# Attention and two expert layers on one core: where the second layer's logits copy, one unit's row splits and one unit's transposes stand in the queues

## The chip, the cores and the metric

The kernel runs on one core of a Trainium2 chip. Its time is the device time of one execution in microseconds (us). Before the change three runs gave 878.62, 884.17 and 881.64 us, median 881.64.

## What is computed

Attention over 4 batches, 12 heads, 448 positions and 64 channels, with q and k normalised by their root mean square, gives 1792 token rows of 768 values. Two mixture-of-experts layers follow. Each routes every token to one of 8 experts (768 to 1024 to 768) by the largest logit:

```python
    logits = x @ w_gate                       # second layer: + modality_bias[modality_id]
    e_idx = np.argmax(logits, axis=1)
...
        h = np.maximum(x[mask] @ w1[e], 0.0)
        ye = h @ w2[e]
        out[mask] = gate_w[mask, None] * eom[mask, e, None] * ye   # second layer: without eom
```

## The kernel before the change

**Units.** After attention the tokens stand in a table in order of expert. The kernel works in *units*: up to N tokens of one expert. The first layer has `ua`, `ub` and seven units P0 to P6 with N = 304, 288, 256, 240, 224, 208, 192 (`CAPS`). The second layer has `e2`, `e3` and then `seq`: four wide units B0 to B3 with N = 304 and two remainder units S0, S1 with N = 64, in the order B0, B1, B2, S0, B3, S1. A branch (`If`, L1022) stands in the first of them.

**One unit** (`halves`, L416). Phase 1 has eight steps `fb` 0 to 7: 18 matmuls each (`mm3`, L378: three products of 16-bit halves for 6 slices of the 768 inputs) from the transposed rows `XT` and the first weight (`w1h`, `w1l`) into a PSUM tile `pl`; then ScalarE writes `hh` (L381) and VectorE the remainder `hl` (L382), which also frees the PSUM tile (three in all). Phase 2 has six steps `db` 0 to 5 of 24 matmuls from `hh`, `hl` and the second weight (`w2h`, `w2l`); step db ends in a copy to `yt` (L456), and the transposes of a step (`ytrans`, `pty`, L444) follow one step later in `after`. In the first layer `after` also adds the next layer's logits into the PSUM tile `lgT` (L452).

**Weights.** SyncE loads fp32 slices (`r` for w1, `raw`, `r2a`, `r2b` for w2; L317). ScalarE casts the high half (L310), VectorE subtracts for the low half (L311). A load waits until the earlier slice in its buffer has been split.

**Rows.** GpSimd gathers a unit's token rows into `xr` (L357). `xsplit` (L358) casts the high half on ScalarE into `XS` (L361) and subtracts the low half on GpSimd or VectorE (L362). `xtrans` (L363) is a transposing DMA from `XS` to `XT` on SyncE's queue (L365); a remainder unit has its own `XTx`. `XPLAN` (L501) says at which step of a unit the *next* unit's rows are split on the default engine VectorE (`s`), split with the subtraction on GpSimd (`p`) or transposed (`t`); `late` names the row of that table. With `late=0` all rows are split at step 0 on GpSimd and transposed at step 7.5, between the phases.

**The end of a unit runs inside the next one.** `post` (L468) is a generator: step `do(0)` of the next unit first works through the plan and then takes one piece of it: the last `after`, the scatter of the finished rows (`scatter`, L383, GpSimd), and in the first layer the first piece of `route2` (L485): the copy of `lgT` to `lt` in SBUF (L487, ScalarE). The next pieces follow one step each: logits `lg` on TensorE (L490), the routing arithmetic on VectorE (L494 to L160), the table's scatter (L163).

**Order.** `pin` fixes every engine's instructions in program order. So an instruction that waits holds up all that stand behind it on its engine or queue.

Of the kernel before, what the change touches and what calls it, by code (L numbers as in the profile page):

```python
# [24 lines left out]
def bc(ap, shape):  # L25
    return ap.to_broadcast(shape)

class Moe:
# [366 lines left out]
    def unit(self,u,nx=None,fx=None,side=None,late=0,mid=None,fast={},now=False,fp=0,fr=7,**kw):  # L395

        gen=self.gen(); side=dict(side or {})
        plan=XPLAN[late] if nx is not None else {}
        def do(s):
            if fx is not None and s==fp: self.fetch_pay(fx)  # L400
            for k,t in plan.get(s,()):
                if t<nx.ntl:
                    if k=="t": self.xtrans(nx,t)
                    else: self.xsplit(nx,t,self.nc.gpsimd if k=="p" else None)
            if fx is not None and s==fr: self.fetch_rows(fx)
            for _ in range(fast.get(s,1)): next(gen,None)
            for f in side.pop(s,()): f()
        warm=nx is not None and not nx.same
        for _ in self.halves(u,nx,warm,do,fx,cut=mid is not None,**kw): mid([k for s in plan if s<MID for k in plan[s]])
        for _ in gen: pass  # L410
        for s in sorted(side): do(s)
        if now:
            self.flush()
            if fx is not None: self.fetch_idx(fx)
        elif fx is not None and fr>KF+KD: self.fetch_rows(fx)
    def halves(self,u,nx,warm,do,fx=None,early=True,wfb=None,cut=False):  # L416
        nc=self.nc; N=u.N; pay=self.pays[u.slot]; ntl=u.ntl
        if wfb is None: wfb=0 if N<=128 else 3 if nx is not None and not nx.same and nx.x else 5
        (w2h,w2l),XT=self.planes(u),self.xplane(u)
        xh,xl,hh,hl=[t[:,:,:N] for t in (XT[:,0],XT[:,1].bitcast(BF16),self.hh,self.hl)]  # L420
        r=self.width(u); w1h,w1l=self.planes1(u)
        def w2s():
            self.expert(nx)
            for k in range(KF): self.load_w2(nx,k)
        soon=warm and u.x and not u.same
        for fb in range(KF):
            mid=cut and fb==MID
            if not u.same and not u.x and not mid: self.split_w2(fb,u)
            p=(self.lgp if mid else self.ps.tile([128,512],F32,name="pl1",tag="pl"))[:,:N]
            self.mm3(p,[(w1h[:,k,ts(fb,128)],w1l[:,k,ts(fb,128)],xh[:,k],xl[:,k]) for k in range(KD)],r)  # L430
            if mid: yield; self.split_w2(fb,u)
            do(fb)
            self.relu(p,hh[:,fb],hl[:,fb])
            if soon and fb==1: w2s()
            if warm and nx.x:
                self.expert(nx); self.load_w2(nx,fb)
                if fb>=4: self.split_w2(fb-4,nx)
            if warm and fb==wfb and not nx.w1: self.bring(nx)
        if soon: self.split_w1(0)
        do(7.5)  # L440
        if warm and (u.same or not u.x) and not nx.x: w2s()
        def ytrans(d):
            q=self.pt.tile([128,4,128],F32,name="pty",tag="pt")[:,:ntl]
            for t in range(ntl): nc.tensor.transpose(q[:,t,:],self.yt[:,d,ts(t,128)],self.ident)  # L444
            if u.L.nxt is not None and ntl==2:
                for t in range(ntl): nc.scalar.mul(self.yr[:,t,ts(d,128)],q[:,t],pay[:,t,1:2])
            else: nc.vector.tensor_tensor(out=self.yr[:,:ntl,ts(d,128)],in0=q,in1=bc(pay[:,:ntl,1:2],[128,ntl,128]),op=ALU.mult)  # L447
        Y={}
        def after(d):
            ytrans(d)  # L450
            if u.L.nxt is not None:
                for j in range(2): nc.tensor.matmul(self.lgp[:2*E,:N],u.L.nxt["wgs"][:,d],Y.pop((d,j)),start=(d,j)==(0,0),stop=(d,j)==(KD-1,1))  # L452
        for db in range(KD):
            p=self.ps.tile([128,512],F32,name="pl2",tag="pl")[:,:N]
            self.mm3(p,[(w2h[:,k,ts(db,128)],w2l[:,k,ts(db,128)],hh[:,k],hl[:,k]) for k in range(KF)],r)
            nc.scalar.copy(self.yt[:,db,:N],p)  # L456
            if u.L.nxt is not None:
                yh,yl=[self.st.tile([128,self.NM],F32R,name=n,bufs=2)[:,:N] for n in ("yh","yl")]
                nc.scalar.copy(yh,p); nc.vector.tensor_tensor(out=yl,in0=p,in1=yh.bitcast(F32),op=ALU.subtract)
                Y[db,0],Y[db,1]=yh,yl  # L460
            if db>0: after(db-1)
            if warm and not nx.px: self.warm2(db,None,soon)
            if warm and nx.x:
                if 0<db<5: self.split_w2(db+3,nx)
                if fx is not None and db>2: self.bring(fx,*((0,2),(2,3),(3,4))[db-3])
            do(KF+db)
        if fx is not None and early and not fx.same and not (u.x and fx.x): self.bring(fx,*((4,KD) if warm and nx.x else ()))
        def post():  # L468
            after(KD-1)
            self.scatter(u)  # L470
            if u.L.nxt is not None: yield from self.route2(u,pay[:,:ntl,1:2])
            yield
        self.post=post
# [10 lines left out]
        for k in ((1,) if soon and db==0 else ((0,1),(2,),(3,),(4,),(5,),())[db]): self.split_w1(k,eng=eng if k in (1,3) else None)  # L484
    def route2(self, u, scale):  # L485
        nc=self.nc; R=128; nx=u.L.nxt; sp=self.lp; sm=self.sm; ntl=u.ntl; yt=self.yt; pay=self.pays[u.slot][:,:ntl]; iv=self.ivs[u.slot][:,:ntl]
        nc.scalar.copy(self.lt[:2*E,:u.N],self.lgp[:2*E,:u.N])  # L487
        yield
        lg=sm.tile([128,ntl,E],F32,name="lg2",tag="tp")
        for t in range(ntl): nc.tensor.matmul(lg[:,t,:],self.lt[:2*E,ts(t,128)],self.fold[:2*E],start=True,stop=True)  # L490
        T=lambda n,s=(),dt=F32: sp.tile([128,self.ntl,*s],dt,name="r2_"+n,tag="r2_"+n)[:,:ntl]
        l=T("l",(E,)); b=T("b",(E,)); b2=T("b2",(2,E))
        sh=[128,ntl,E]
        nc.vector.tensor_tensor(out=b2,in0=bc(nx["bias"].unsqueeze(1),[128,ntl,2,E]),in1=bc(pay[:,:,2:4].unsqueeze(3),[128,ntl,2,E]),op=ALU.mult)  # L494
        nc.vector.tensor_tensor(out=b,in0=b2[:,:,0],in1=b2[:,:,1],op=ALU.add)
        nc.vector.tensor_tensor(out=l,in0=lg,in1=bc(scale,sh),op=ALU.mult)
        nc.vector.tensor_tensor(out=l,in0=l,in1=b,op=ALU.add)
        yield
        yield from self.route_g(sp,sm,l,ntl,R,nx["ohsum"],nx["ord"],iv=iv,pay=pay,tag="tp",lag=True)

XPLAN={5:{1:[("s",1),("t",0)],2:[("s",2),("t",1)],3:[("t",2)]},7:{9:[("s",0),("t",0)]},4:{0:[("p",0)],2:[("t",0),("t",1),("t",2)]},6:{1:[("t",0),("t",1),("t",2)]},0:{0:[("p",0),("p",1),("p",2)],7.5:[("t",0),("t",1),("t",2)]},3:{3:[("s",0)],4:[("s",1)],5:[("s",2)],7.5:[("t",0),("t",1),("t",2)]},  # L501
1:{8:[("s",0),("s",1),("s",2),("t",0),("t",1),("t",2)]},
    2:{7.5:[("s",0),("s",1),("s",2),("t",0),("t",1),("t",2)]},None:{10:[("s",0),("t",0)]}}
class LazyUnit:
# [329 lines left out]
def body_full(tc,q,k,v,g_q,g_k,wg,wog,w1,w2,mod,wg2,bias2,v1,v2,out,stop=False,O=None):  # L834
    nc=tc.nc
    with ExitStack() as ctx:
        M=Moe(tc,ctx)
# [120 lines left out]
        def stepper(name):  # L958
            def f():
                if name not in S: S[name]=F[name]()  # L960
                next(S[name],None)
            return f
# [18 lines left out]
        sides={1:{KF+j:[stepper("table1")] for j in range(6)},2:{7:[stepper("pick2")]*2,**{j:[stepper("pick2")] for j in range(8,14)}},3:{7:[stepper("pick3")]*2,**{j:[stepper("pick3")] for j in range(8,14)}}}  # L981
        for g in range(7): M.unit(P[g],nx=P[g+1],fx=P[g+2],side=sides.get(g),late=0 if g else 3)
        e2,e3=S["e2"],S["e3"]
# [14 lines left out]
            yield from M.chunks(S["s2"],lp,ns,off3,c,NS,E)  # L998
        F.update(table2=table2,table3=table3)
        t2=stepper("table2")  # L1000
        M.unit(e2,nx=e3,side={j:[t2] for j in (7,8,9,10,11)})
        M.unit(e3,nx=B0,fx=S["B"][1],side={0:[lambda: M.fetch_pay(B0)],2:[lambda: M.fetch_rows(B0)],**{KF+i:[stepper("table3")] for i in range(6)}},late=1,fp=8,fr=9)
        seq=S["B"][:3]+[S["S"][0],S["B"][3],S["S"][1]]
        (be,nbi),(se,nsi)=S["b2"],S["s2"]
# [28 lines left out]
            return f  # L1033
        def known(): S["over"]=load(over,E+G2+G1)
        def px(t): return lambda: M.xsplit(seq[4],t,nc.gpsimd)
        sides={0:{0:[more],3:[known]},2:{KF+3+t:[px(t)] for t in range(3)},4:{KF+1:[nc.gpsimd.drain]}}
        for u in seq: u.own=True
        for j,u in enumerate(seq):
            nx,fx=seq[j+1] if j<5 else None,seq[j+2] if j<4 else None
            M.unit(u,nx=nx,fx=fx,side=sides.get(j),late={2:4,3:6,4:4}.get(j,0),mid=others(u,nx,fx) if j==0 else None)  # L1040
        M.flush()
        pin(tc,mark)

# [28 lines left out]
```

## Time and profile before

| | |
|---|---|
| median of three runs | 881.64 us |
| the profiled execution | 877.29 us |
| its span | 875.6 us |
| PE busy | 817.9 us (93%) |
| VectorE (DVE) busy | 649.3 us (74%) |
| ScalarE (ACT) busy | 545.0 us (62%) |
| GpSimd (POOL) busy | 389.9 us (45%) |
| mean granted TensorE clock | 0.98 |

The profiled execution's 877.29 us is 1.69 us over its span and 4.35 us under the median of the three runs. Attention takes about the first 300 us of the span, the first expert layer the stretch to about 610 us, the second the rest.

### The profile page before, as it was taken

Reading aid. Unit: us, or ns where it says so; the run is one execution under the profiler, and the core shown is the slowest. Engines: PE = TensorE matmul, PEld = TensorE weight load, DVE = VectorE, ACT = ScalarE, POOL = GpSimd, SP = SyncE. Lnnn points to the kernel's source line nnn. Section 1 sums busy time; section 2 is a strip of 40 time slices with the busy share of each in tenths; the row PEclk is TensorE's granted clock in tenths of the full one; section 3 lists DMA queues with packets and bytes.
Section 4 is the critical chain, followed back from the end, with each engine's and each line's share of the span. In section 5 each row is a group of like instructions: output and inputs, shape, how many; then the busy total and the mean of one; then the engine's idle time right before and its main releaser. Section 6 shows DMA issues by size and latency. Waiting matters only on the chain. (4 is left out here: it accounts for less than half of the span.)

```text
span 875.6 us, 23286 instructions
## 1 busy us (share of the span) xinstructions
PE 817.9 (93%) x8881; PEld 640.0 (73%) x8898; DVE 649.3 (74%) x1302; ACT 545.0 (62%) x1039; POOL 389.9 (45%) x397
## 2 busy tenths in 40 slices
PE   4698999998998899899999999999999999999897
PEld 1265666665665588777889999988677768878676
DVE  6689889888778775786797767776676846577674
ACT  4577777776776654655556686776545535456563
POOL 5677777876776623131424333344402524024301
PEclk9799999998999989999999999999999999999999
DMA  5567665766465482979486797898677759896961
GB/s 137 130 152 183 162 155 162 201 161 163 114 172 142 143 229 77 278 290 326 105 321 145 275 320 201 249 348 239 204 251 280 235 108 332 192 315 207 291 245 52
DMA packets 142137, 181.42 MB, mean 207 GB/s; under 512 B 71944, under 2 KB 109592, under 8 KB 142016
## 3 DMA queue, kind: packets, MB, share of 16 engines
q1 hardware_dynamic: 134048, 157.06, 62.9%
q0 software_dynamic: 6656, 22.32, 7.8%
q8 instruction: 71, 1.16, 0.6%
q10 hardware_dynamic: 1312, 0.47, 0.2%
q14 instruction: 50, 0.41, 0.2%
HBM read 129.73 MB, written 23.94 MB: 176 GB/s over the span
## 5 line engine op out<-in xcount | busy, mean ns | idle before, releaser
L378 PE MATMUL pl<-XT,w1h 128*128 128x304 f16 (+6 forms) x1236 | 210.5, 275 | 4.9 <-PEq L1022 2.0
L378 PE MATMUL pl<-hh,w2h 128*128 128x304 f16 (+7 forms) x720 | 194.4, 275 | 0.0
L378 PE MATMUL pl<-hh,w2l 128*128 128x304 f16 (+7 forms) x720 | 194.1, 274 | 0.0
L378 PE MATMUL pl<-hl,w2h 128*128 128x0 bf16 x720 | 187.9, 264 | 3.0 <-DVE hl L382 3.0
L378 PE MATMUL pl<-XT,w1l 128*128 128x304 f16 (+6 forms) x618 | 172.5, 279 | 0.0
L680 POOL TENSOR_TENSOR plo<-p 128x448 f16<-128x448 f32 x142 | 140.3, 1005 | 56.1 <-ACT p L677 52.4
L378 PEld LDWEIGHTS <-w1h 128*128 128x128 f16 x1536 | 134.5, 98 | 27.4 <-ACTq L1022 2.3
L378 PEld LDWEIGHTS <-w2h 128*128 128x128 f16 x1440 | 134.0, 98 | 24.6 <-issue 1.4
L311 DVE TENSOR_TENSOR w1l<-r,w1h 128x1024 bf16<-128x1024 f32 x90 | 109.7, 1233 | 46.5 <-ACT w1h L310 46.5
L456 ACT COPY yt<-pl 128x304 f32<-128x304 f32 (+8 forms) x102 | 36.6, 358 | 117.2 <-PE pl L378 117.2
L362 POOL TENSOR_TENSOR XS<-xr,XS 128x768 bf16<-128x768 f32 (+5 forms) x27 | 46.8, 1749 | 130.4 <-ACT XS L361 100.6
L381 ACT ACTIVATE hh<-pl 128x304 f16<-128x304 f32 (+8 forms) x135 | 49.1, 364 | 81.0 <-PE pl L378 69.5
L677 ACT ACTIVATE p<-pst,eb 128x896 f32<-128x896 f32 (+1 forms) x96 | 86.5, 911 | 14.8 <-PE pst L673 13.9
L310 ACT CAST w1h<-r 128x1024 f16<-128x1024 f32 x90 | 93.5, 1056 | 0.1
L690 PE MATMUL av<-vv,p 128*128 128x65 f16 (+1 forms) x768 | 89.8, 199 | 1.8 <-ACT xrow L702 1.8
L690 PEld LDWEIGHTS <-p 128*128 128x128 bf16 (+1 forms) x768 | 73.5, 102 | 20.8 <-issue 15.0
L692 PE MATMUL av<-vv,plo 128*128 128x65 f16 (+1 forms) x768 | 88.0, 196 | 0.6 <-DVE plo L680 0.6
L691 PE MATMUL av<-vv,p 128*128 128x64 f16 (+1 forms) x768 | 88.5, 198 | 0.0
L654 DVE TENSOR_REDUCE m<-psm 128x2 f16<-128x896 f32 x70 | 76.0, 1086 | 9.1 <-PE psm L649 7.3
L378 PEld LDWEIGHTS <-w1l 128*128 128x128 bf16 x768 | 74.1, 98 | 11.8
L378 PEld LDWEIGHTS <-w2l 128*128 128x128 bf16 x720 | 70.3, 98 | 16.7 <-issue 4.1
L382 DVE SCALAR_TENSOR_TENSOR hl<-pl,hh 128x304 bf16<-128x304 f32 (+8 forms) x135 | 53.5, 398 | 34.8 <-ACT hh L381 34.4
(328 smaller groups left out, 1806.3 us busy)
## 6 DMA issues: line engine op xcount, KB each, us to landing
r<-in_moe_w_dram SPq DMA_DIRECT2D x96, 512.0 KB, 8.9
raw<-in_moe_w_dram SPq DMA_DIRECT2D x64, 384.0 KB, 5.9
r2a<-in_moe_w_dram SPq DMA_DIRECT2D x32, 384.0 KB, 6.8
r2b<-in_moe_w_dram SPq DMA_DIRECT2D x32, 384.0 KB, 8.9
T<-Z SPq DMA_DIRECT2D x48, 224.0 KB, 3.8
T<-Z SPq DMA_DIRECT2D x48, 112.0 KB, 2.9
yd<-zero SPq DMA_DIRECT2D x14, 384.0 KB, 3.1
rv<-in_v_dram SPq DMA_DIRECT2D x24, 192.0 KB, 4.2
```

What stands on the lines that cost most here:

```text
L310: if part!=1: nc.scalar.copy(h,t)
L311: if part!=0: (eng or nc.vector).tensor_tensor(out=l,in0=t,in1=h,op=ALU.subtract)
L362: if part!=0: (eng or nc.vector).tensor_tensor(out=self.XS[:m,t,1].bitcast(BF16),in0=x,in1=h,op=ALU.subtract)
L378: self.nc.tensor.matmul(o,a,b,start=i==0,stop=i==tot-1); i+=1
L381: nc.scalar.activation(h,p,AF.Relu)
L382: nc.vector.scalar_tensor_tensor(out=l,in0=p,scalar=0.0,in1=h,op0=ALU.max,op1=ALU.subtract)
L654: if t<3: nc.vector.tensor_reduce(m[:,t:t+4:3],p[:,:,:S],axis=AX.X,op=ALU.max,negate=True)
L677: self.nc.scalar.activation(self.d["P",i][:,self.u(kt)],p[:,:nn,:S],AF.Exp,bias=self.eb,scale=0.125)
L680: eng.tensor_tensor(out=self.d["L",i][:,u],in0=P[:,u],in1=self.hi(P)[:,u],op=ALU.subtract)
L690: nc.tensor.matmul(o,hh,w[:,0:65],start=kt==0,stop=False)
L691: nc.tensor.matmul(o[:,0:64],hh,w[:,65:129],start=False,stop=False)
L692: nc.tensor.matmul(o,ll,w[:,0:65],start=False,stop=kt==3)
```

## The change

It has three parts.

1. `post` copies `lgT` to `lt` itself, as a piece of its own, and `do(0)` takes that piece *before* the plan. The last `after` comes with it. A later call takes the scatter and, in the first layer, route2's first piece, as before.
2. `e2` gets `late=3` in place of 0: the rows of `e3` are split at steps 3, 4 and 5 with the subtraction on VectorE, instead of at step 0 on GpSimd. The transposes stay at step 7.5.
3. B3's rows are split on GpSimd at steps db 2, 3 and 4 of B2 instead of 3, 4 and 5, and each tile is transposed one step after its split, still in B2. Before, the three transposes stood at step 1 of S0 (`XPLAN[6]`); S0's plan is now empty (`XPLAN[8]`).

```diff
@@ unit
         def do(s):
             if fx is not None and s==fp: self.fetch_pay(fx)
+            if s==0: next(gen,None)
             for k,t in plan.get(s,()):
@@ halves
         def post():
             after(KD-1)
+            if u.L.nxt is not None: nc.scalar.copy(self.lt[:2*E,:N],self.lgp[:2*E,:N])
+            yield
             self.scatter(u)
             if u.L.nxt is not None: yield from self.route2(u,pay[:,:ntl,1:2])
             yield
@@ route2
-        nc.scalar.copy(self.lt[:2*E,:u.N],self.lgp[:2*E,:u.N])
         yield
@@ XPLAN (of the line, the entry that differs)
-6:{1:[("t",0),("t",1),("t",2)]}
+8:{}
@@ body_full
-        M.unit(e2,nx=e3,side={j:[t2] for j in (7,8,9,10,11)})
+        M.unit(e2,nx=e3,side={j:[t2] for j in (7,8,9,10,11)},late=3)
...
-        sides={0:{0:[more],3:[known]},2:{KF+3+t:[px(t)] for t in range(3)},4:{KF+1:[nc.gpsimd.drain]}}
+        def tx(t): return lambda: M.xtrans(seq[4],t)
+        sides={0:{0:[more],3:[known]},2:{KF+2:[px(0)],KF+3:[px(1),tx(0)],KF+4:[px(2),tx(1)],KF+5:[tx(2)]},4:{KF+1:[nc.gpsimd.drain]}}
...
-            M.unit(u,nx=nx,fx=fx,side=sides.get(j),late={2:4,3:6,4:4}.get(j,0),mid=others(u,nx,fx) if j==0 else None)
+            M.unit(u,nx=nx,fx=fx,side=sides.get(j),late={2:4,3:8,4:4}.get(j,0),mid=others(u,nx,fx) if j==0 else None)
```

ScalarE at the start of P6 (N = 192), before. `XS<-xr` are the casts of e2's three row tiles, `yr` the end of P5, `hh` P6's first phase.

```order
L310 CAST w2h<-raw_118 128x768
L361 CAST XS<-xr_78 128x768
L361 CAST XS<-xr_79 128x768
L361 CAST XS<-xr_80 48x768
L446 ACTIVATE yr<-pty,pay_84 128x128 x2
L487 COPY lt<-lgT 16x208
L381 ACTIVATE hh<-pl_10098 128x192
```

The same place now:

```order
L310 CAST w2h<-raw_118 128x768
L447 ACTIVATE yr<-pty,pay_84 128x128 x2
L471 COPY lt<-lgT 16x208
L361 CAST XS<-xr_78 128x768
L361 CAST XS<-xr_79 128x768
L361 CAST XS<-xr_80 48x768
L381 ACTIVATE hh<-pl_10098 128x192
```

The casts of the rows now stand behind `yr` and `lt`, and `hh` stays last. The same holds at the starts of P1 to P5, with two row tiles (in P1 and P2 without `yr`, which VectorE writes for three tiles).

GpSimd at the start of e2, before (`xr` are e3's rows, `yd` the rows that P6 has finished):

```order
L357 DMA xr_80<-yd,idx_87 48x768
L362 TENSOR_TENSOR XS<-xr_78,XS 128x768
L362 TENSOR_TENSOR XS<-xr_79,XS 128x768
L362 TENSOR_TENSOR XS<-xr_80,XS 48x768
L387 DMA yd<-yr,idx_85 1792x768 x2
```

VectorE in phase 1 of e2 now, steps 2 to 5:

```order
L382 SCALAR_TENSOR_TENSOR hl<-pl_10713,hh 128x304
L311 TENSOR_TENSOR w2l<-raw_119,w2h 128x768
L362 TENSOR_TENSOR XS<-xr_78,XS 128x768
L382 SCALAR_TENSOR_TENSOR hl<-pl_10750,hh 128x304
L311 TENSOR_TENSOR w2l<-r2a,w2h 128x768
L362 TENSOR_TENSOR XS<-xr_79,XS 128x768
L382 SCALAR_TENSOR_TENSOR hl<-pl_10776,hh 128x304
L311 TENSOR_TENSOR w2l<-r2a,w2h 128x768
L362 TENSOR_TENSOR XS<-xr_80,XS 48x768
```

The three subtractions have left GpSimd's queue, where the scatter of P6 stood behind them, and stand between the `hl` and `w2l` of VectorE. ScalarE's three casts have moved to the same steps.

SyncE's queue at the end of B2, before. The loads `r_0` to `r_5` of B3's first weight stand in a row; these are the last of them and what follows (`pay` is for S1, `raw` is B3's second weight):

```order
L317 DMA r_5_75<-in_moe_w_dram 128x1024
L321 TENSOR_LOAD s2gi
L321 ISA x2
L345 ISA
L345 DMA pay_81<-o_1132 64x4
L365 DMA_TRANSPOSE XT<-XS 128x12x128 x2
L365 DMA_TRANSPOSE XT<-XS 128x12x48
L317 ISA
L317 DMA raw_118<-in_moe_w_dram 128x768
```

The same place now, from `r_1` on:

```order
L317 DMA r_1_71<-in_moe_w_dram 128x1024
L365 DMA_TRANSPOSE XT<-XS 128x12x128
L317 ISA
L317 DMA r_2_72<-in_moe_w_dram 128x1024
L365 DMA_TRANSPOSE XT<-XS 128x12x128
L317 ISA
L317 DMA r_3_73<-in_moe_w_dram 128x1024
L365 DMA_TRANSPOSE XT<-XS 128x12x48
L317 ISA
L317 DMA r_4_74<-in_moe_w_dram 128x1024
L317 ISA
L317 DMA r_5_75<-in_moe_w_dram 128x1024
```

The transposes now stand ahead of the loads `r_2`, `r_3` and `r_4`, which they had stood behind.

## Rows read from the trace of the kernel before

**Rows 1.** Waits of PE, whole span: us in total, times, longest.

```profile
PE pl L378 <- DVE hl L382: 4.0, 9, 0.7
...
PE lg L490 <- ACT lt L487: 3.8, 3, 2.2
```

**Rows 2.** Timeline of PE at e2's start: start, duration, in brackets idle before.

```profile
615.28 0.61 PE L490 MATMUL lg<-fold,lt 16*128 16x8 f32 x4 [2.17 <-ACT lt L487]
```

**Rows 3.** Timeline of PE: phase 2 of P3 and of P6 waits for hl.

```profile
503.93 0.24 PE L378 MATMUL pl<-hl,w2h 128*128 128x0 bf16 x1 [0.35 <-DVE hl L382]
...
595.95 0.24 PE L378 MATMUL pl<-hl,w2h 128*128 128x0 bf16 x1 [0.66 <-DVE hl L382]
```

**Rows 4.** Timeline of ACT: start of P3, and the casts at P6.

```profile
487.79 1.58 ACT L361 CAST XS<-xr 128x768 f16<-128x768 f32 x2
489.25 0.63 ACT L446 ACTIVATE yr<-pty,pay 128x128 f32<-128x128 f32 x2
489.76 0.34 ACT L487 COPY lt<-lgT 16x256 f32<-16x256 f32 x1
...
579.17 2.31 ACT L361 CAST XS<-xr 128x768 f16<-128x768 f32 x3
```

**Rows 5.** Timeline of PE: the last transposes, at P3 and at P6.

```profile
488.01 0.38 PE L444 MATMUL pty<-ident,yt 128*128 128x128 f32 x2
...
579.17 0.38 PE L444 MATMUL pty<-ident,yt 128*128 128x128 f32 x2
```

**Rows 6.** Timeline of POOL at the start of P3.

```profile
488.74 3.27 POOL L362 TENSOR_TENSOR XS<-xr,XS 128x768 bf16<-128x768 f32 x2 [9.21 <-ACT XS L361]
```

**Rows 7.** Timeline of DVE in phase 1 of P3.

```profile
491.12 1.70 DVE L311 TENSOR_TENSOR w2l<-raw,w2h 128x768 bf16<-128x768 f32 x1 [0.31 <-ACT w2h L310]
...
493.66 0.95 DVE L311 TENSOR_TENSOR w2l<-raw,w2h 128x768 bf16<-128x768 f32 x1
```

**Rows 8.** Timeline of ACT at the start of e2.

```profile
612.95 1.57 ACT L361 CAST XS<-xr 128x768 f16<-128x768 f32 x2 [1.30 <-DMA xr<-yd,idx]
...
614.93 0.29 ACT L487 COPY lt<-lgT 16x192 f32<-16x192 f32 x1
```

**Rows 9.** Timeline of PE at the start of e2: the last logits.

```profile
610.52 0.25 PE L452 MATMUL lgT<-yl,wgs 128*16 128x192 f32 x1
```

**Rows 10.** Stretches: length, PE, PEld, DVE, ACT, POOL busy (instructions), PE clock, DMA, GB/s.

```profile
616.00:632.70 16.70, 16.70 (x134) 12.67 (x133) 13.18 (x38) 7.65 (x15) 6.24 (x5) 1.00 0.48 166
821.00:822.00 1.00, 1.00 (x6) 0.59 (x5) 0.78 (x2) 0.31 (x1) 0.00 (x0) 0.50 1.03 402
```

**Rows 11.** Timeline of PE at B3's start.

```profile
820.14 0.68 PE L378 MATMUL pl<-XT,w1h 128*128 128x304 f16 x2 [1.92 <-DMA XT<-XS]
```

**Rows 12.** Timeline of POOL in B2 and S0.

```profile
803.22 2.08 POOL L362 TENSOR_TENSOR XS<-xr,XS 128x768 bf16<-128x768 f32 x1 [9.43 <-ACT XS L361]
806.58 3.78 POOL L362 TENSOR_TENSOR XS<-xr,XS 128x768 bf16<-128x768 f32 x2 [1.28 <-ACT XS L361]
```

**Rows 13.** Timeline of SyncE's queue: loads of B3's w1, then the transposes.

```profile
792.99 13.74 SPq L317 DMA_DIRECT2D r<-in_moe_w_dram  x6
...
808.19 7.70 SPq L365 DMA_TRANSPOSE XT<-XS  x3
```

**Rows 14.** Timeline of DVE in S0 and B3.

```profile
816.16 0.29 DVE L447 TENSOR_TENSOR yr<-pty,pay 128x128 f32<-128x128 f32 x1 [0.81 <-DMA out_dram<-yr,idx]
...
820.37 1.22 DVE L311 TENSOR_TENSOR w1l<-r,w1h 128x1024 bf16<-128x1024 f32 x1
```

**Rows 15.** Timeline of ACT at B3's start.

```profile
817.16 1.09 ACT L310 CAST w1h<-r 128x1024 f16<-128x1024 f32 x1
...
824.10 0.42 ACT L381 ACTIVATE hh<-pl 128x304 f16<-128x304 f32 x1 [0.85 <-PE pl L378]
```

**Rows 16.** DMA issues from 785 to 830 us: KB each, median us to landing.

```profile
r<-in_moe_w_dram SPq DMA_DIRECT2D x6, 512.0 KB, 5.3
...
XT<-XS SPq DMA_TRANSPOSE x3, 8.9
```

More of the change, by code (lines that the diff above doesn't have):

```diff
@@ L499, in route2 @@
         yield from self.route_g(sp,sm,l,ntl,R,nx["ohsum"],nx["ord"],iv=iv,pay=pay,tag="tp",lag=True)
-XPLAN={5:{1:[("s",1),("t",0)],2:[("s",2),("t",1)],3:[("t",2)]},7:{9:[("s",0),("t",0)]},4:{0:[("p",0)],2:[("t",0),("t",1),("t",2)]},6:{1:[("t",0),("t",1),("t",2)]},0:{0:[("p",0),("p",1),("p",2)],7.5:[("t",0),("t",1),("t",2)]},3:{3:[("s",0)],4:[("s",1)],5:[("s",2)],7.5:[("t",0),("t",1),("t",2)]},
+XPLAN={5:{1:[("s",1),("t",0)],2:[("s",2),("t",1)],3:[("t",2)]},7:{9:[("s",0),("t",0)]},4:{0:[("p",0)],2:[("t",0),("t",1),("t",2)]},8:{},0:{0:[("p",0),("p",1),("p",2)],7.5:[("t",0),("t",1),("t",2)]},3:{3:[("s",0)],4:[("s",1)],5:[("s",2)],7.5:[("t",0),("t",1),("t",2)]},
 1:{8:[("s",0),("s",1),("s",2),("t",0),("t",1),("t",2)]},
```

## The prediction

> **What bounds the kernel now.** I read the page first: PE is busy 93% of the span, so only work or waits on PE's path can move the time, and after that the waits of PE. Two groups of them bear on the change: 3.8 us in three waits for `lt`, and 4.0 us in nine for `hl` [rows 1]. The longest wait for `lt`, 2.17 us, stands at e2's start [rows 2]; the other two (1.6 us together) stand at P5's and P6's starts.
>
> Then the timeline, stage by stage. Phase 2 of P3 waits 0.35 us for VectorE's last `hl`, that of P6 0.66 us; P4 and P5 lie between [rows 3]. So in these four units VectorE sets the end of phase 1: its chain runs without a gap from the second step on. What PE wins back earlier in such a unit it loses to that `hl`, and what delays VectorE there delays PE in full. The other place is B3's start, where PE waits 1.92 us for the transposed rows [rows 11].
>
> **Part 1, the copy of the logits ahead of the casts.** At P3 the two casts start at 487.79; `yr` and `lt` follow at 489.25 and 489.76 [rows 4]. Now `yr` and `lt` come first. They need the last transposes, which end at 488.39 [rows 5]. Two `yr` take 0.51 us (489.25 to 489.76), `lt` about 0.25 (from 489.76 to where `hh` is begun), so the first cast starts at 488.39 + 0.75 = 489.14, 1.35 us later. GpSimd's two subtractions, which end at 488.74 + 3.27 = 492.01 [rows 6], follow it. That matters because VectorE's `w2l` at 491.12 takes 1.70 us where the same operation a step later takes 0.95 [rows 7]: it ends 0.81 us after GpSimd does, as if it had waited for GpSimd's end. So GpSimd's end starts VectorE's chain, and the chain has no slack. I charge P3 with the whole 1.35 us.
>
> At P6 the casts start at 579.17 [rows 4], the transposes end at 579.55 [rows 5]: 579.55 + 0.75 − 579.17 = 1.13. P4 and P5 by the same arithmetic come to 1.29 and 1.20. Sum 1.35 + 1.29 + 1.20 + 1.13 = 5.0. In P2 the casts move 2.1 us, but `hl` has some 1.8 us of room there; I take 0.2. P1 and the earlier units are covered by their room. Part 1 in P1 to P6: **+5.2 us**. Its own gain there, the two shorter waits for `lt` (1.6 us), is worth nothing, since `hl` comes last. Bounds: 0, if GpSimd's delay finds VectorE busy with something else; 7, if P2 pays in full.
>
> At e2 the copy is free to start when the last logits end, 610.52 + 0.25 = 610.77 [rows 9]; before, it stood at 614.93 behind casts that waited for the gather of rows [rows 8]. The copy thus ends near 611.4, 3.8 us sooner, and the wait of 2.17 us [rows 2] is gone entirely: **−2.2 us**. The bounds are 0, if something else of the same length is late there, and 2.2.
>
> **Part 2, e3's rows on VectorE.** It adds three subtractions of 0.95 us (the duration of the like `w2l`, [rows 7]), 2.85 us, to e2's phase 1. In that stretch VectorE is busy 13.18 of 16.70 us [rows 10], so 3.52 us are free and PE didn't wait for `hl`. I cost it at nothing; the cover is thin, and gone if the freed start moves phase 1 closer to VectorE. Then up to 2.2 us return as a wait for the last `hl`. GpSimd loses 5 us of work off the path; the casts cost ScalarE nothing that PE waits for.
>
> **Part 3, B3's rows.** Before, the splits run at 803.22 and from 806.58 to 810.36 [rows 12], and the three transposes issue from 808.19 on, for 7.70 us, behind all six loads [rows 13]. One step of B2 is about 3.36 us (806.58 − 803.22), so the first split now starts near 799.9, the second and third where the first and second stood, at 803.2 and 806.6; at 1.9 to 2.1 us each they end near 802, 805.3 and 808.4. With the slowest landing in the trace, 8.9 us [rows 16], the last transpose is in at 808.4 + 8.9 = 817.3, before S0's last matmul (820.14 − 1.92 = 818.2 [rows 11]). The 1.92 us go; what is late next is the low half of B3's first weight: VectorE's last `w1l` ends at 820.37 + 1.22 = 821.59 [rows 14]. Ahead of it `yr` waited 0.81 us for the scatter [rows 14], which GpSimd now issues about 1.3 us sooner; so 820.78. Three matmuls of 0.13 us behind it end the first step at 821.2. Before, `hh` of that step began at 824.10 [rows 15]: after the wait the granted clock stood at 0.50, the 1.2 GHz level [rows 10]. The gain is 824.1 − 821.2 = **−2.9 us**.
>
> The cost is in SyncE's queue. The loads `r_2` to `r_5`, issued until 792.99 + 13.74 = 806.73 before [rows 13], now stand behind transposes that wait for GpSimd. The third can't issue before 808.4, so `r_5` goes at about 812. With 5.3 us [rows 16] it lands at 817.3; its cast stood at 817.16 [rows 15], and the chain of `w1l` gives it another microsecond or two. I charge nothing, and nothing for `pay` and the second weight's loads, which stay behind. As the upper bound, `r_5` waits for the last transpose to land and then takes 5.3 us: 817.3 + 5.3 = 822.6, cast 1.09, `w1l` 1.22, matmuls 0.39: 825.3, that is +1.2.
>
> This last order is also what a page speaks of. The Trainium skill, "DMA: Bandwidth & Descriptors", section "Queues, rings and completion order", says that on each DMA engine the descriptors of one queue are consumed in ring order, so a load behind a transpose can't overtake it. By it `r_5` would land some 1.4 us after the third transpose, at 818.7, and the first step would end at 821.4: a gain of 2.7 instead of 2.9. No run here shows it yet.
>
> **Sum.** 5.2 − 2.2 − 2.9 = +0.1. The profiled execution took 877.29, so 877.4; it lies 4.35 under the median of the runs shown, 881.64, and I forecast against that median: **881.7**.
>
> **Rivals.**
>
> 1. *The later casts cost VectorE nothing.* VectorE's `w2l` gets in between GpSimd's two subtractions, and the chain fits. For it: P1's and P2's chains have room. Against it: the 1.70 against 0.95 in P3 [rows 7], and waits for `hl` at all four ends. −2.2 − 2.9 = −5.1: 876.5.
> 2. *Slower: the queue.* The place is SyncE between `r_1` and `r_5`; the price is `r_5` landing up to 822.6. It decides from about 818.5 on, where the last `w1l` no longer hides it. Then part 3 gives +1.2 instead of −2.9: +4.2, 885.8. For it: the transposes take 7.70 us of the queue's time [rows 13]. Against it: DMA has free time in S0.
> 3. *Part 3 changes nothing:* the clock falls there anyway, or the weight comes as late as the rows did. 5.2 − 2.2 = +3.0: 884.6. For it: `w1l` ends only 1.45 us after PE's present restart at 820.14.
> 4. *Part 2 takes e2's gain back:* +2.3, 883.9.
>
> **Numbers.** Chances: forecast 0.50, rivals 0.17, 0.15, 0.13, 0.05. The range takes in all of them, 876.5 to 885.8, and something over a microsecond at either end, since the three runs of before alone lie 5.6 us apart: **875 to 887**. One per cent, 8.8 us, is about what a measurement can tell from no change; no case reaches it by itself. Faster by more than 1%: 0.04; within it: 0.91; slower: 0.05.
>
> **What would show it.** In the profile after: no wait for `lt` at e2; the first cast of P3 some 1.3 us later within the unit and its `w2l` of the second step longer by as much, with `hl` waits of 1.5 to 2 us at the starts of phase 2 of P3 to P6 in place of 0.2 to 0.7 (if they stay as they are, rival 1 holds); an e2 without a wait for `hl`; at B3 no wait for the rows, a granted clock of 1.00, and `r_5` landing before 818.5 on the old time. The forecast is wrong if VectorE's chain in P3 to P6 has room that the waits don't show, or if B3's start keeps its wait under another name.

## The result and the profile after

Six runs of the changed kernel gave a median of 890.07 us, six of the kernel before 879.15: a ratio of 1.0139, 95% interval 1.011 to 1.0169. A second comparison (below) gave 1.0091, interval 1.0061 to 1.012. The change makes the kernel slower by about 1%. The forecast was no change (881.7, range 875 to 887); the time measured lies 3 us above that range.

The profiled execution took 889.20 us, its span 887.5. Read first the waits of PE (total, times, longest), against [rows 1]:

```profile
PE pl L378 <- DVE hl L382: 16.4, 14, 7.4
```

The waits for `hl` rose from 4.0 to 16.4 us. Of the rise, 7.4 us are one wait in S0, and 5.0 lie in P2 to P6 (2.4 before, 7.4 now). The waits for `lt` (3.8 us) are gone, and so is the wait for the rows at B3. The timeline of PE tells where the new ones stand (start, duration, idle before in brackets); one row each of P3, P4, P5, P6, and the longest, in S0:

```profile
501.62 0.34 PE L378 MATMUL pl<-XT,w1h 128*128 128x240 f16 x2 [0.69 <-DVE hl L382]
...
534.46 0.34 PE L378 MATMUL pl<-XT,w1h 128*128 128x224 f16 x2 [0.94 <-DVE hl L382]
...
565.96 0.33 PE L378 MATMUL pl<-XT,w1h 128*128 128x208 f16 x2 [1.19 <-DVE hl L382]
...
598.11 0.32 PE L378 MATMUL pl<-XT,w1h 128*128 128x192 f16 x2 [1.97 <-DVE hl L382]
...
827.44 0.19 PE L378 MATMUL pl<-hl,wxh 128*128 128x0 bf16 x1 [7.40 <-DVE hl L382]
```

**The start of P3,** all engines, against [rows 4], [rows 6] and [rows 7]:

```profile
495.43 0.34 ACT L471 COPY lt<-lgT 16x256 f32<-16x256 f32 x1
495.68 1.56 ACT L361 CAST XS<-xr 128x768 f16<-128x768 f32 x2
496.59 3.23 POOL L362 TENSOR_TENSOR XS<-xr,XS 128x768 bf16<-128x768 f32 x2 [8.93 <-ACT XS L361]
...
498.25 2.39 DVE L311 TENSOR_TENSOR w2l<-raw,w2h 128x768 bf16<-128x768 f32 x1 [0.31 <-ACT w2h L310]
```

P3 now begins at 492.75 (486.28 before), so the casts stand 2.93 us into the unit, 1.42 later than before. `w2l` of the second step starts 0.66 us later within the unit, takes 2.39 us instead of 1.70, and ends at 500.64, 0.82 us after GpSimd (499.82), just as before (0.81).

**The start of e2,** PE, against [rows 2]: the logits no longer wait.

```profile
624.56 0.61 PE L492 MATMUL lg<-fold,lt 16*128 16x8 f32 x4
```

**S0,** VectorE and SyncE's queue, against [rows 13] and [rows 14]:

```profile
819.30 0.20 DVE L351 TENSOR_SCALAR iv<-pos,s2gc 128x1 f32<-128x1 f32 x1
827.09 0.16 DVE L352 TENSOR_TENSOR idx<-pay,iv 128x1 int32<-128x1 f32 x1 [7.58 <-DMA pay<-o]
827.17 0.22 DVE L382 SCALAR_TENSOR_TENSOR hl<-pl,hh 128x64 bf16<-128x64 f32 x1
```

```profile
809.46 1.47 SPq L365 DMA_TRANSPOSE XT<-XS  x1
811.18 0.71 SPq L317 DMA_DIRECT2D r<-in_moe_w_dram  x1
812.92 2.19 SPq L365 DMA_TRANSPOSE XT<-XS  x1
815.35 0.71 SPq L317 DMA_DIRECT2D r<-in_moe_w_dram  x1
816.38 1.21 SPq L365 DMA_TRANSPOSE XT<-XS  x1
817.83 1.13 SPq L317 DMA_DIRECT2D r<-in_moe_w_dram  x2
819.79 0.55 SPq L345 DMA_DIRECT2D pay<-o  x1
```

The same load of `pay` before the change:

```profile
807.53 0.55 SPq L345 DMA_DIRECT2D pay<-o  x1
```

This is the cause in three steps. `pay`, the 64 rows of the table that S1's gather needs, is issued behind `r_5`, which stands behind transposes that wait for GpSimd. It goes at 819.79, 5.0 us after S0's first product (814.80); before, it went 0.3 us after it (807.53 and 807.24). VectorE works out S1's row numbers (`idx`, L352) at step 7 of S0's first phase and waits 7.58 us for it. S0's last `hl` stands behind `idx` on VectorE, and phase 2 needs that `hl`.

B3's start itself came out as forecast: no wait for the rows, and the granted clock at 1.00, the 2.4 GHz level, where it stood at 0.50 [rows 10]. Stretches of the changed kernel (columns as there), the second in S0's phase 2 after the wait:

```profile
834.00:835.00 1.00, 1.00 (x9) 0.76 (x8) 1.00 (x3) 0.59 (x1) 0.00 (x0) 1.00 0.37 110
...
828.00:829.00 1.00, 1.00 (x22) 0.94 (x20) 0.61 (x2) 1.00 (x3) 0.62 (x1) 0.50 1.04 418
```

**Where the 11.9 us between the two spans lie.** A unit is counted from PE's first product in it to that of the next:

| us | P0's start | P0 to end | P2 to P6 | e2 | S0 + B3 | S1 |
|---|---|---|---|---|---|---|
| before | 372.58 | 502.99 | 156.18 | 42.24 | 53.06 | 15.27 |
| changed | 378.83 | 508.64 | 161.45 | 40.00 | 57.76 | 14.91 |

6.25 us lie ahead of P0, and all of them ahead of `ua` (which starts at 317.38 and 323.69), in the attention, which the change doesn't touch. From P0 on: +5.27 in P2 to P6, −2.24 in e2, +4.70 in S0 and B3, −1.71 in B0 (which holds the branch), −0.36 in S1. B0's part isn't the change's: a second trace of the kernel before (below) has 41.25 us there, like the changed kernel's 41.27, and not 42.98. The 4.70 are 7.40 for the new wait, less 1.92 for the rows' wait and 1.45 in B3, plus 0.7 in the rest of S0.

### The profile page after: what moved, and what is told of

Same layout as the page of the kernel before. It is cut to its first block, busy times and chain, and to the rows that moved or that the text cites. A ratio compares the mean times of both kernels' runs of the same rounds, so it can differ in the third digit from the quotient of the medians.

```text
span 887.5 us, 23272 instructions
## 1 busy us (share of the span) xinstructions
PE 822.2 (93%) x8881; PEld 643.0 (72%) x8898; DVE 655.9 (74%) x1305; ACT 546.0 (62%) x1039; POOL 382.1 (43%) x394
## 5 line engine op out<-in xcount | busy, mean ns | idle before, releaser
L378 PE MATMUL pl<-XT,w1h 128*128 128x304 f16 (+6 forms) x1236 | 208.0, 273 | 8.5 <-DVE hl L382 5.7
L362 POOL TENSOR_TENSOR XS<-xr,XS 128x768 bf16<-128x768 f32 (+5 forms) x24 | 41.4, 1740 | 125.9 <-ACT XS L361 108.7
L692 PEld LDWEIGHTS <-p 128*128 128x128 bf16 (+1 forms) x768 | 74.3, 103 | 21.2 <-issue 15.4
L693 PEld LDWEIGHTS <-p 128*128 128x128 bf16 (+1 forms) x768 | 75.5, 104 | 2.0 <-issue 1.0
```

Of the source, the lines that this page charges most:

```text
L362: if part!=0: (eng or nc.vector).tensor_tensor(out=self.XS[:m,t,1].bitcast(BF16),in0=x,in1=h,op=ALU.subtract)
L378: self.nc.tensor.matmul(o,a,b,start=i==0,stop=i==tot-1); i+=1
L692: nc.tensor.matmul(o,hh,w[:,0:65],start=kt==0,stop=False)
L693: nc.tensor.matmul(o[:,0:64],hh,w[:,65:129],start=False,stop=False)
```

## The experiments

**The parts one by one.** Four kernels on one chip. In all four TensorE's small products of S0 and S1 had four or five gaps, most of 0.4 to 0.6 us and some 0.75 us apart (S1 took 18.3 to 19.7 us in place of 15), and the kernel before ran at a median of 887.24 beside them; so the ratios within the set count, and stage against stage within it. (P4 to P6 have a few such waits too, of 0.4 to 0.9 us.) None of the four came out at its expected time from P0's start to the end: 510.3, 507.0, 514.4 and 508.6 us against about 506, 500.8, 505.7 and 500.5.

Part 1 alone (`e2` with late=0, B3's rows as before):

> Part 1 alone: the logits copy ahead of the casts everywhere; e2's rows plan and B3's rows as before the change. Theory: the later casts move GpSimd's row subtractions, and with them VectorE's chain, by 1.1 to 1.6 us in each of P2 to P6, +5.3 us in all, and the wait for lt at e2 goes, -2.2: from P0's start to the end +3 us against before (503.0). Rival, that the loss in P2 to P6 needs part 2 or 3: about -2. If the slower attention of the changed kernel (P0 starts at 378.8 in place of 372.6) comes from part 1, P0 starts near 379 here.

Ratio 1.0047 (1.0014 to 1.0081). P2, P3, P5 and P6 took 34.79, 32.94, 30.66 and 31.24 us, as in the changed kernel, so the loss there needs neither part 2 nor 3 (P4 took 32.25 against 31.63, which isn't explained). The wait for `lt` at e2 is gone; e2 took 40.56, as PE waits 0.39 us for `hl` there. P0 started at 378.67.

Part 2 alone:

```diff
-        M.unit(e2,nx=e3,side={...})
+        M.unit(e2,nx=e3,side={...},late=3)
```

> Part 2 alone: e3's rows split on VectorE at steps 3 to 5 of e2. Theory: lt at e2 no longer stands behind the casts, since these have left step 0; -2.2 us from P0's start to the end (503.0 before), and P2 to P6 as before. Rival, that only the copy's move wins it: 0. P0 starts within a few us of 372.6 if the attention's time is not the change's.

Ratio 0.9986 (0.9954 to 1.0018), which leaves the sign open. In the trace e2 takes 39.99 us against 42.24, and the wait for `lt` is gone. But this trace alone doesn't show that part 2 won it. Part 3 alone and part 3 with `pay` early (next) have neither part 1 nor part 2; the first has the same row as part 2 alone, the second waits 1.88 us:

```profile
621.37 0.61 PE L490 MATMUL lg<-fold,lt 16*128 16x8 f32 x4
...
620.53 0.61 PE L490 MATMUL lg<-fold,lt 16*128 16x8 f32 x4 [1.88 <-ACT lt L487]
```

In the fourteen traces the wait is absent from all eight with part 1 or part 2, and lasts 0 to 2.17 us in the six with neither (0.8 on average): the casts ahead of the copy wait for the gather of the rows. So either part takes the wait away, and what that is worth changes from run to run. P2, P3 and P4 are as before (34.58, 31.59, 30.34).

Part 3 alone, and part 3 with `pay` early:

> Part 3 alone: B3's rows split and transposed sooner. Theory: pay for S1 is issued on SyncE after the transposes and r_5, lands some 7 us after VectorE's idx wants it, and hl of S0 stands behind idx: a PE wait of 7 us for hl in S0, the rows' wait of 1.9 and the half clock after it gone, +2.7 us from P0's start to the end. My forecast before the result: -2.9. Rival, that the late loads r_2 to r_5 hold S0: the wait is the same with pay early (next kernel).

```diff
-2:{KF+2:[px(0)],...
+2:{KF+1:[lambda: M.fetch_pay(seq[5])],KF+2:[px(0)],...
-M.unit(u,nx=nx,fx=fx,...
+M.unit(u,nx=nx,fx=fx,...,fp=99 if j==3 else 0)     # no second fetch in S0
```

> Part 3 alone, with pay for S1 issued on SyncE at step db 1 of B2, ahead of the loads of B3's first weight. Theory: no wait for hl in S0; the last weight slice lands about 1 us later than its chain wants, so B3's first step ends 2 to 3 us sooner than before the change: -2.5 us from P0's start to the end, and 5 us under the kernel with part 3 alone. Rival, the loads r_2 to r_5 themselves are too late: S0 or B3's start waits 3 us or more for w1h or w1l, 0 to +2 us.

Part 3 alone: ratio 1.0065 (1.0031 to 1.0098). With `pay` early: 0.9975 (0.9942 to 1.0008). The same instruction on VectorE, first without and then with the early issue:

```profile
825.23 0.16 DVE L352 TENSOR_TENSOR idx<-pay,iv 128x1 int32<-128x1 f32 x1 [5.23 <-DMA pay<-o]
```

```profile
819.91 0.16 DVE L352 TENSOR_TENSOR idx<-pay,iv 128x1 int32<-128x1 f32 x1
```

S0 takes 19.83 and 14.58 us, B3 38.70 in both; PE's wait for `hl`, 4.71 us without the early issue, is gone with it. Moving one load of 1 KB takes 5.25 us out of S0, and with it all of part 3's loss; the late loads `r_2` to `r_5` themselves, which both kernels have, hold nothing of that size (in a faster S0 the last of them does cost 0.9 us: see the version with parts 2 and 3 and `pay` early, below). My rival 2 had the right queue and the wrong victim. The gain over a kernel without part 3 is small in this set (S0 and B3 took 53.6 with part 1 or part 2 alone, 53.28 here), since the slow S0 hides B3's rows anyway.

**Both kernels again.**

> The kernel before, profiled a second time. If the attention's time (P0 starts at 372.6 in the first trace, 378.8 in that of the changed kernel, 376 to 379 with one part alone) is a matter of when TensorE's granted clock falls after the same waits, it starts P0 elsewhere than at 372.6 here, up to 379; if the change slows the attention, at 372.6 within 1 us. From P0's start to the end 503 us, and some 2 us more in S0 and S1 if the gaps of TensorE seen there in the runs with one part alone belong to the chip or the run.

> The changed kernel again. By the parts measured alone (part 1 +4.2, part 3 +5.8, with part 2 adding nothing since part 1 wins the same wait) +8 to +10 us against before; by the stages of the two traces +5.7; by the first comparison +10.9.

The kernel before, a second time: P0 starts at 375.51, and from there to the end it takes 501.47 us. P2 to P6 agree with the first trace to 0.06 us. Two waits don't: the logits at e2 wait 0.67 in place of 2.17, and the rows at B3 2.32 in place of 1.92:

```profile
616.79 0.61 PE L490 MATMUL lg<-fold,lt 16*128 16x8 f32 x4 [0.67 <-ACT lt L487]
...
820.19 0.68 PE L378 MATMUL pl<-XT,w1h 128*128 128x304 f16 x2 [2.32 <-DMA XT<-XS]
```

The changed kernel: 887.83 (11 runs) against 879.51 (28 runs), ratio 1.0091 (1.0061 to 1.012); P0's start 377.37, P0 to end 508.83, P2 to P6 161.24, S0 and B3 57.87. So the stages from P0 on cost 5.7 us in the first pair of traces and 7.4 in the second, and 7.4 in both when B0 is left out.

P0's start differs by run, not by edit. In the fourteen traces it lies between 372.1 and 378.8, and the two last versions below, whose code is the same up to P0's second phase, stand at 372.25 and 376.96. The waits there are alike; TensorE's granted clock is not. Stretches of the first 300 us, before and changed (length, busy times of PE, PEld, DVE, ACT, POOL with instructions, PE clock, DMA, GB/s):

```profile
80.00:100.00 20.00, 17.72 (x227) 12.05 (x226) 18.80 (x30) 14.69 (x27) 15.39 (x16) 1.00 0.71 180
...
0.00:300.00 300.00, 267.31 (x3328) 174.94 (x3329) 247.50 (x437) 210.35 (x382) 213.01 (x263) 0.97 0.62 157
```

```profile
80.00:100.00 20.00, 17.72 (x205) 11.61 (x204) 17.32 (x28) 12.90 (x22) 14.71 (x14) 0.91 0.76 190
...
0.00:300.00 300.00, 266.43 (x3244) 171.98 (x3245) 245.22 (x431) 208.10 (x378) 211.50 (x262) 0.95 0.62 154
```

In the first pair both wait 1.98 us at 87 to 88 us; the changed kernel goes on at the 1.2 GHz level for a while, the other doesn't. The mean of the first 300 us is 0.97 against 0.95. The second profile of the kernel before has 0.95 too. All fourteen traces fall in line: by their clock records TensorE stood at the 1.2 GHz level for 20 to 41 us ahead of `ua`, and `ua` starts at 316.7 to 317.4 us with 20 to 27 of them, at 320.1 to 321.2 with 34, at 321.6 to 322.1 with 38 and at 323.5 to 323.7 with 41 (27 in the first trace of before, 41 in that of the changed kernel). Why the clock falls in one execution and not in the next isn't shown. The medians differ by 10.9 and 8.3 us, 3.5 and 0.9 more than the 7.4 of the stages; the attention's spread is large enough for the rest, and no trace shows another place.

**What part 1 costs, by taking GpSimd's work away.** Part 1 alone, with

```diff
+        c=slice(0,8) if u.L.nxt is not None and eng is not None and u.N<=240 else slice(None)
-        (eng or nc.vector).tensor_tensor(out=self.XS[:m,t,1].bitcast(BF16),in0=x,in1=h,...)
+        (eng or nc.vector).tensor_tensor(out=self.XS[:m,t,1].bitcast(BF16)[:,c],in0=x[:,c],in1=h[:,c],...)
```

> Part 1 alone, and GpSimd's subtraction of the rows of P3 to P6 cut to 8 of 768 columns (their low halves are left out; the casts on ScalarE stay where part 1 puts them). P6 itself, in which e2's rows are split in full, is the control. Theory (GpSimd's late end holds VectorE's chain): the steps' waits for hl in P3 to P5 go, P3, P4, P5 last 31.6, 30.3, 29.5 us or less (as before or sooner) in place of 32.9, 31.6 to 32.2 and 30.7, and w2l of the second step takes 0.95; P6 stays at 31.2 to 31.4. Rival (ScalarE's new order delays hh and hl, GpSimd is no part of it): P3 to P5 stay at 32.9, 31.6, 30.7.

P3, P4, P5 take 31.50, 30.15, 29.21 us, all under before (31.59, 30.34, 29.49); the control P6 takes 31.24, as with part 1. The `w2l` of the second step in P3:

```profile
496.68 0.96 DVE L311 TENSOR_TENSOR w2l<-raw,w2h 128x768 bf16<-128x768 f32 x1 [0.31 <-ACT w2h L310]
```

ScalarE's order is part 1's, and the loss is gone: it came wholly through GpSimd's subtractions. The Trainium skill, "SBUF — State Buffer", section "Who interferes with whom", says that a VectorE instruction with two inputs in SBUF contends with a GpSimd instruction that reads SBUF. The trace agrees: 2.39 us beside GpSimd, 0.96 without.

**Row splits sooner, on the kernel before.**

```diff
+        for g in range(6): ... side[12] of P[g] += split of P[g+2]'s rows on GpSimd
-        M.unit(P[g],...,late=0 if g else 3)
+        M.unit(P[g],...,late=9 if g else 3)      # 9: only the transposes at 7.5
```

> Opposite of part 1 in its side effect, on the kernel before: the row tiles of each unit of P2 to P6 and of e2 are split on GpSimd two steps sooner, at step db 4 of the unit before, rather than at step 0. Theory (GpSimd's end starts VectorE's chain in P3 to P6): GpSimd is done before w2l of the second step, that takes 0.95 and not 1.70 us, the waits for hl in P3 to P6 (2.4 us in all) fall, and lt at the starts of P5, P6 and e2 comes sooner: -2 to -4 us from P0's start to the end. Rival, VectorE's chain has another cause, and only the wait for lt shrinks: 0 to -1.

Ratio 0.9987 (0.9952 to 1.0023); P2 to P6 156.58 against 156.18. The mechanism held (P4 29.94, P5 28.52; `w2l` 0.96 at P3), but the casts were put ahead of the last copy to `yt`, and PE waited for that at the next unit's start. ScalarE at the end of P2, and PE:

```profile
486.95 0.83 ACT L361 CAST XS<-xr 128x768 f16<-128x768 f32 x1 [1.09 <-issue]
488.61 0.83 ACT L361 CAST XS<-xr 96x768 f16<-96x768 f32 x1 [0.83 <-DMA r2b<-in_moe_w_dram]
489.35 0.36 ACT L456 COPY yt<-pl 128x256 f32<-128x256 f32 x1
```

```profile
489.77 0.44 PE L444 MATMUL pty<-ident,yt 128*128 128x128 f32 x2 [0.83 <-ACT yt L456]
```

Both casts stood idle first (1.09 and 0.83 us), as the rows' gather had been issued only 7.6 and 7.9 us before they ran, and the last `yt` stood behind them. At P6's start PE waited 1.98 us in that way, for three casts.

> A version meant to beat both: part 2, part 3 with pay for S1 ahead of the weight loads, and the row tiles of P2 to P6 and e2 split at step db 4 of the unit before; the logits copy stays behind the plan. Sum of the pieces: -2.2 (e2), 0 to -2.5 (B3), -2 to -4 (P3 to P6), so 4 to 9 us under before. Rival: the pieces share one gain (lt at e2), 2 to 4 us under.

Ratio 0.9975 (0.9943 to 1.0007): S0 and B3 51.62, but the same waits for `yt`. Here SyncE has the order of the change with `pay` taken out of it, and S0 runs without its long wait (11.97 us). Now `r_5` shows: ScalarE's cast of it waits, then PE for the low half, and B3 takes 39.65 us in place of 38.70:

```profile
822.66 1.04 ACT L310 CAST w1h<-r 128x1024 f16<-128x1024 f32 x1 [1.81 <-DMA r<-in_moe_w_dram]
...
825.01 0.30 PE L378 MATMUL pl<-XT,w1l 128*128 128x304 f16 x1 [0.78 <-DVE w1l L311]
```

**B3's splits sooner, the queue as before.**

> B3's rows split one step of B2 sooner, and nothing else of part 3: transposes, loads and pay stand on SyncE as before. S0 and B3 together took 53.1 and 54.7 us in two traces of before. If the splits alone hold the transposes: the second and third issue up to 2 us sooner, the wait for the rows falls from 1.9 or 2.3 to under 1 and S0 with B3 takes 51.5 to 52.5. If the queue holds them (the second transpose takes 3.4 us to issue): within 0.5 of before.

Both outcomes missed. S0 and B3 took 55.92 us, PE waited 5.30 for the rows. The three transposes issue as a block, as in [rows 13], and took 9.03 us for it, not 7.70:

```profile
807.57 0.55 SPq L345 DMA_DIRECT2D pay<-o  x1
808.23 9.03 SPq L365 DMA_TRANSPOSE XT<-XS  x3
```

```profile
822.99 0.68 PE L378 MATMUL pl<-XT,w1h 128*128 128x304 f16 x2 [5.30 <-DMA XT<-XS]
```

The last split ended at 808.78, before the second transpose was issued, so the splits aren't what holds the block:

```profile
806.57 2.21 POOL L362 TENSOR_TENSOR XS<-xr,XS 48x768 bf16<-48x768 f32 x1 [1.24 <-ACT XS L361]
```

The block took 6.74 to 9.03 us in the seven traces that have it, and one execution doesn't show that the sooner splits made it longer. One behind each load, as in the changed kernel, the three take 1.47, 2.19 and 1.21. Why a block is slow wasn't tried apart; GpSimd's scatters and the gather for S1 are issued beside it.

**Versions meant to beat both.** Part 2; `pay` at step db 1 of B2; each transpose two loads later than in the change, so that `r_2` and `r_3` go ahead of all three:

```diff
+        M.hook={seq[4]:{3:tx(0),4:tx(1),5:tx(2)}}     # bring: after load r_k, call hook k
```

and the row splits one tile at a step in the last two or three steps of the unit before (for P2's rows too, which the expectation doesn't name).

> A version meant to beat both: part 2; pay for S1 at step db 1 of B2; B3's splits one step sooner, its transposes on SyncE one behind each of the loads r_3, r_4 and r_5; the row tiles of P3 to P6 and e2 split one tile at a step in the last two or three steps of the unit before. No part 1. Sum: P2 to P6 0 to -2.4, e2 -0.7 to -2.2, S0 with B3 -2 to -3 against 53.1 and 54.7: 3 to 7 us under before from P0's start to the end. Rival: casts in the last steps hold the last copy to yt, as where two stood in one step (waits of 0.8 to 2.0 us for it): P2 to P6 +1, and 2 to 4 us under.

Ratio 0.9967 (0.9933 to 1.0001). S0 and B3 took 50.07 us. P2 to P6 took 157.27: P2 35.54 and P5 31.93 paid. In P5 ScalarE's first cast of e2's rows stood idle 3.88 us at the head of its queue, for rows that weren't there. The gathers were issued at 569.87 and after, and took 7.4 us to land (issues, median us to landing):

```profile
xr<-yd,idx POOLq DMA_INDIRECT x3, 7.4
```

```profile
577.76 0.83 ACT L363 CAST XS<-xr 128x768 f16<-128x768 f32 x1 [3.88 <-issue]
```

> The version meant to beat both, with the sooner row splits kept only where they paid: the rows of P4, P5 and P6 (split in the last two steps of P2, P3 and P4); those of P2, P3 and e2 stand at step 0 as before (their sooner splits made P2 0.96 us longer and P5 2.4 us longer). Part 2 and the repaired part 3 as in the version before it. From the stages: P2 34.6, P3 31.2, P4 29.9, P5 29.0 to 29.5, P6 30.2, e2 40.0, S0 with B3 50 to 51: from P0's start to the end 496 to 497 us against 503.0 and 501.5 of the two traces of before, 5 to 7 us under before. Rival: the sooner splits only shift a wait of some 1 us to the next unit: 498 to 499.

871.39 us (6 runs) against 880.45 (11 runs): ratio 0.9896, interval 0.985 to 0.9941. P2 to P6 154.48, e2 40.00, S0 and B3 50.06, P0 to end 496.10. P3, P4, P5 take 31.07, 29.94 and 28.72 us. Its queue at the end of B2, with `pay` long gone:

```profile
802.74 1.51 SPq L367 DMA_TRANSPOSE XT<-XS  x1
804.49 0.84 SPq L317 DMA_DIRECT2D r<-in_moe_w_dram  x1
806.20 2.29 SPq L367 DMA_TRANSPOSE XT<-XS  x1
808.73 0.38 SPq L317 DMA_DIRECT2D r<-in_moe_w_dram  x1
809.65 1.21 SPq L367 DMA_TRANSPOSE XT<-XS  x1
```

## Why the prediction was wrong

- **Part 1 in P2 to P6: right, in mechanism and size.** Forecast +5.2, measured +5.27 and +5.0 (161.45 and 161.24 against 156.18 and 156.24). Unit by unit the forecast was 0.2, 1.35, 1.29, 1.20, 1.13; the trace has 0.22, 1.36, 1.29, 1.19, 1.21. The expected signs were off: PE paid inside phase 1, where `hl` frees the PSUM tiles, and not at the starts of phase 2 (0.2 to 0.7 us there, as before); and P3's `w2l` grew by 0.69 us and not by 1.3, as it also starts 0.66 later. Before, P4 waited 0.18 us there, less than P3, and not between P3 and P6 as the text reads it.
- **The copy at e2: right in mechanism, lucky in size.** −2.24 against the first trace, for −2.2. The price was taken from one execution, and that is the longest such wait in six traces (0 to 2.17 us); in the second trace of before it is 0.67, and the gain −0.74. The stated bounds, 0 to 2.2, hold it.
- **Part 2 at nothing: right.** e2 has no wait for `hl` after. Beside part 1 it even saves 0.56 us: with part 1 alone PE waits 0.39 us for `hl` in e2.
- **Part 3: wrong, and it decides.** Forecast −2.9, measured +4.7 against the first trace of before and +3.1 against the second. The step that failed is the charge of nothing for `pay`, for a reason named there, that `pay` stays behind the loads. It does stay there, and that is the fault: it was pushed back with them, from 0.3 to 5.0 us after S0's start, and the text doesn't ask who reads it. `idx` reads it, S0's last `hl` stands behind `idx`, and PE waits 7.40 us. I followed `r_5` to its reader and stopped one row short in the same queue. At B3 the forecast held: no wait for the rows, and the clock there is back at the 2.4 GHz level, so B3 itself takes 38.70 us, not 40.15.
- **`r_5`: not free either.** The longer S0 hid it. In the version with parts 2 and 3 and `pay` early its cast begins 12.73 us after S0's start (822.66 and 809.93), on the old time at 820.0, where the text had it land at 817.3 and let rival 2 decide from 818.5 on; that costs B3 0.9 us, and S0 with B3 then came to 51.62, 1.4 under the first trace of before and 3.1 under the second. (The 8.9 us of [rows 16] is a median, not the slowest landing.) A wait of 2 us for the rows doesn't always cost the clock, either: with part 1 and the cut subtractions PE waits 2.03 us for them, the granted clock stays at 1.00 and B3 takes 38.72. And the argument against rival 2, free time of the DMA in S0, isn't borne out by the trace of before: over S0 the mean busy share of the DMA engines (next to last figure; columns as in [rows 10]) is 1.11.

```profile
807.24:820.14 12.90, 10.10 (x298) 9.47 (x296) 9.37 (x21) 9.03 (x22) 7.97 (x6) 0.98 1.11 222
```

- **The page on the queue.** The Trainium skill, "DMA: Bandwidth & Descriptors", section "Queues, rings and completion order", has a queue's descriptors consumed in order on each DMA engine (a later one may still finish its write first). I applied it to `r_5` alone. The trace agrees with it for `pay`: 1 KB, read 7.3 us after its issue behind two loads of 512 KB, and no wait once it is issued ahead of them. For `r_5` the text had 818.7 by this rule and 817.3 by its own; 820.0 lies past both.
- **The base.** The median of 881.64 came from three runs; the five sets of runs since put the kernel before at medians from 878.5 to 887.2. P0's start alone moves by 6.7 us from trace to trace. The range allowed a little over a microsecond at either end, for runs that lie 5.6 us apart.

With part 3 at its measured size the sum is 5.2 − 2.2 + 4.7 = +7.7, or 889.3 against the 890.07 measured. That nearness is in part luck: against the 879.15 of the six runs of before, +7.7 gives 886.9, and the rest is of the size of the attention's spread.

## What to carry to other kernels

When a step is moved ahead of others in a queue, list every entry that it passes or pushes back, down to the smallest, and for each the first instruction that reads it and what stands behind that reader on its engine. A small load behind large ones is as late as they are: here 1 KB cost PE 7.4 us. Where two engines get in each other's way, the start of the one off the path can set the end of the other, as GpSimd's did VectorE's in P3, and a copy won ahead of it is paid back. Before a wait is priced, look at it in more than one execution.

## What the runs showed of the hardware

- A transposing DMA issued directly behind another held SyncE's queue: three in a row took 6.7 to 9.0 us to issue (seven traces), and 4.9 to 5.0 in all with a load between them (the other seven).
- After the same wait of 1.98 us near 87 us, TensorE went on at the 2.4 GHz level in one execution and at 1.2 GHz in another; P0's start moved by up to 6.7 us between executions whose attention code is the same.
- In the set of four kernels TensorE's products of up to 64 columns ran with four or five gaps, most of 0.4 to 0.6 us and some 0.75 us apart, in S0 and S1 alike; S1 took 18.3 to 19.7 us, and 14.9 to 15.3 in all traces of the other sets. Its cause wasn't found.
